# Linear attention into a gated feed-forward layer: k and v of batches 1 and 2 laid out like those of batches 3 to 7

## The chip, the core and the metric

The kernel runs on one core of one Trainium2 chip. The metric is the device time of one execution in microseconds, given as the median of several runs. A profile is one further execution, recorded by the hardware; its times count from the first instruction.

The core has TensorE (PE: matmuls; PEld is its weight load), VectorE (DVE), ScalarE (ACT), GpSimd (POOL) and SyncE (SP). Loads and stores run on 16 DMA engines. In this kernel they are issued from two queues, GpSimd's and SyncE's; only GpSimd's loads also convert float32 to bf16.

## The reference: what is computed

```python
batch, n_heads, seq, head_dim = (8, 8, 576, 64)
theta = pi / 2 * arange(S) / S
phi(x) = concatenate([relu(x) * cos(theta), relu(x) * sin(theta)])   # 64 -> 128 features per token
kv  = einsum('bhsf,bhsd->bhfd', phi(k), v)         # 128 x 64 per head
z   = sum over s of phi(k)
out = einsum('bhsf,bhfd->bhsd', phi(q), kv) / (einsum('bhsf,bhf->bhs', phi(q), z) + 1e-06)

x   = out as 4608 tokens x 512                      # heads side by side
xn  = x / sqrt(mean(x * x) + 1e-06) * rms_g
y   = (silu(xn @ w_gate) * (xn @ w_val)) @ w_out    # 512 -> 1536 -> 512
```

All inputs and the output are float32. The matmuls of the kernel run in bf16.

## The kernel before

Everything is written out by hand in one order per engine (`tc.manual_schedule()`): what stands earlier in the program is issued earlier on its engine, and waits are added only for data and for buffers.

**The feed-forward part** sets the frame. There are nine blocks of 512 tokens, run in the order 0 to 6, 8, 7; block 8 collects the last 64 tokens of each batch. A block has twelve steps (n = 0 to 11). Each multiplies by one 128-column slice of the gate and of the value weights (`half_mm`, L556, into PSUM banks psG and psV), applies silu on ScalarE (L570) and the product on VectorE (L571). Then come four output steps (n = 12 to 15; `out_mm`, L574), followed by the store. Block 0 is cut into smaller units, since its inputs arrive one after another (`unit_mm`, L643). After it, `out_first` runs block 0's output steps with batch 1's attention between the matmuls.

**The attention of batch b** is prepared while the block before it runs. A table of slots says after which step what is done: `at(block, step, where, function, ...)`, with "pe", "mid", "pre" and "post" for the place in the step. For each batch:

- `load_kv` (L107) and `load_q` load k, v and q into a ring of five raw buffers of 128 x 2560 float32.
- `k_phi` (L299) maps k, with the cos half on VectorE (L294) and the sin half on ScalarE (L292), into `kp5`, or into `kp`, which is another view of the same memory.
- `v_cast` (L369) converts v to bf16 into `vv` or `vv5`, each with a column of ones, which gives z.
- `kvz_pe` (L382) multiplies the mapped k by v; `kvz_evac` copies the result out of PSUM.
- `q_phi` and transposes give q with its features on the partitions. Batch 1's first transposes are on TensorE (L363), later ones are DMAs of SyncE's queue (L346).
- `nd_pe` (L449) gives numerator and denominator; `nd_post`, `x_sq`, `x_norm` and `x_tr_dma` (L540) divide, normalize and transpose into the block's input.

**Two layouts of k and v.** `wide(b)` chooses, and is true for batches 3 to 7.

- The nine-token layout (batches 0 to 2): two heads share the 128 partitions, 64 partitions each, and a partition holds nine consecutive tokens of four heads. One load has 128 x 4 pieces of 2,304 bytes. `kvz_pe` needs 4 x 9 x 2 = 72 matmuls with 64 rows (L394); each pair works on the lower and the upper half of the partitions.
- The five-token layout (batches 3 to 7): a partition holds five consecutive tokens of all eight heads, so 115 partitions hold 575 tokens, and the 576th is alone on partition 115. One load has 116 x 8 pieces of 1,280 bytes, issued as two DMAs: rows 0 to 111, then rows 112 to 115 (`KM = 112`; L115). `kvz_pe` needs 4 x 5 x 2 = 40 matmuls with 116 or 115 rows (L387).

Batch 0 has code of its own (`vv0`, `kv0_pe` L430, `z0_pe`), and it uses the nine-token layout directly.

**What sets the order around batches 1 and 2.** GpSimd's queue issues, in this order: q0's first half, v0 in two parts, q0's second half, four pieces of the gate and value weights, k1 (L228), the rest of these weights, q1, v1 (L699), w_out in three parts, k2 (after step 8 of block 0), v2 (step 10). SyncE's queue issues k0 in two parts (L150), and then nothing until batch 1's x is transposed (L540, at 45.9 us). From there on it carries all loads of batches 3 to 7, transposes and stores. Batch 1's k is mapped after steps 5, 6 and 7 of block 0, and its v is cast on GpSimd after step 9 (heads 0 to 3) and on VectorE in step 10 (heads 4 to 7). `kvz_pe(1)` stands in step 11, behind the gate product. Batch 2's k map has four slots (`KCS`, or `KCS5` for the five-token layout) from the output steps of block 0 to step 1 of block 1; its `kvz_pe` is in step 3 of block 1.

Of the kernel before, what the change touches and what calls it, by code (L numbers as in the profile page):

```python
# [10 lines left out]
BF16 = mybir.dt.bfloat16  # L11
# [6 lines left out]
def kernel(  # L18
# [11 lines left out]
    nc = tc.nc  # L30
    B, H, S, D = q.shape
    DM = H * D
    DFF = moe_w_gate.shape[1]
    P = 128
    TB = 512
    HP = H // 2
    NC = S // 64
    NC5 = 5
    KP = S // NC5 + 1
# [3 lines left out]
    E = D + 1  # L43
# [3 lines left out]
    V, A, G = nc.vector, nc.scalar, nc.gpsimd  # L47

    ctx.enter_context(tc.manual_schedule())
    one = ctx.enter_context(tc.tile_pool(name="one", bufs=1))  # L50
# [19 lines left out]
    def kv_rows(src, b, hps):  # L70
        return src[b, 2 * hps[0] : 2 * hps[1], :, :].rearrange(
            "(hp hh) (s c) d -> (hh s) hp (c d)", hh=2, c=NC
        )

    def wide(b):
        return b > 2

    def rows_of(c):
        return KP if c == 0 else KP - 1

    def kv_rows5(src, b, r0, r1):
        part = src[b, :, 0 : NC5 * (KP - 1), :].rearrange(
            "h (p c) d -> p h (c d)", c=NC5
        )[r0 : min(r1, KP - 1)]
        return bass.AP(part.tensor, part.offset, [[NC5 * D, r1 - r0]] + list(part.ap)[1:])
# [6 lines left out]
    def raw_tile(which, b):  # L92
        if (which, b) not in raw:
            t = ring.tile([P, H * NC5 * D], FP32, name="raw", tag="raw")
            raw[(which, b)] = t
        return raw[(which, b)]

    def raw_kv(which, b):
        t = raw_tile(which, b)
        if wide(b):  # L100
            return t[:, :].rearrange("p (h e) -> p h e", h=H)
        return t[:, 0 : HP * NC * D].rearrange("p (hp e) -> p hp e", hp=HP)
# [4 lines left out]
    def load_kv(which, b, hps=(0, HP), eng=nc.sync):  # L107
        src = k if which == "k" else v
        if not wide(b):
            return eng.dma_start(  # L110
                out=raw_kv(which, b)[:, hps[0] : hps[1], :], in_=kv_rows(src, b, hps)
            )
        last = KP if b < B - 1 else KP - 1
        for r0, r1 in ((0, KM), (KM, last)):
            eng.dma_start(  # L115
                out=raw_kv(which, b)[r0:r1, :, :], in_=kv_rows5(src, b, r0, r1)
            )
        if last < KP:
            eng.dma_start(
                out=raw_kv(which, b)[last:KP, :, :].rearrange("p h (c d) -> p h c d", d=D),  # L120
                in_=src[b, :, S - 1 : S, :].rearrange("h s d -> s h d").unsqueeze(2)
                .to_broadcast([1, H, NC5, D]),
            )
# [99 lines left out]
    for i in range(3):  # L223
        m, e = math.frexp(left)
        part.append(math.ldexp(round(m * 256), e - 8))
        left -= part[i]
        G.memset(eps_rows[32 * i : 32 * i + 32, :], part[i] / 32)
    load_kv("k", 1, eng=G)  # L228
    load_w(wg, moe_w_gate, 8, NNT)

# [34 lines left out]
    def cos_of(c):  # L265
# [3 lines left out]
    kp = kp5[:, :, :, :].rearrange("p c h f -> p (c h f)")[:, 0 : NC * HP * F].rearrange(  # L269
        "p (c hp f) -> p c hp f", c=NC, f=F  # L270
    )
    vv = one.tile([P, HP, NC, E], BF16, name="vv")
    vv5 = one.tile([P, H, NC5, E], BF16, name="vv5")
    G.memset(vv[:, :, :, D:E], 1.0)
    G.memset(vv5[:, :, :, D:E], 1.0)
    qpT = one.tile([P, H, TB], BF16, name="qpT")
    xnT = [one.tile([P, NDT, TB], BF16, name=f"xnT{i}") for i in range(2)]
# [6 lines left out]
    def copy(eng, o, i):  # L284
        if eng is A:
            A.copy(out=o, in_=i)  # L286
        else:
            eng.tensor_copy(out=o, in_=i)  # L288
# [10 lines left out]
    def k_phi(eng, b, c, part, hps=(0, HP)):  # L299
        o = slice(0, D) if part == 0 else slice(D, F)  # L300
        f = cos_of if part == 0 else sin_of
        if wide(b):
            rows = rows_of(c)
            src = raw_kv("k", b)[0:rows, :, c * D : (c + 1) * D]
            phi(eng, kp5[0:rows, c, :, o], src, f(14 + c)[0:rows, :])
            return
        src = raw_kv("k", b)[:, hps[0] : hps[1], c * D : (c + 1) * D]
        phi(eng, kp[:, c, hps[0] : hps[1], o], src, f(c))
# [58 lines left out]
        copy(eng, qpT[:, :, j * P : (j + 1) * P], dst)  # L367

    def v_cast(eng, b, hps=(0, HP)):  # L369
        if wide(b):  # L370
            src = raw_kv("v", b).rearrange("p h (c d) -> p h c d", d=D)
            hs = slice(2 * hps[0], 2 * hps[1])
            return copy(eng, vv5[0:KP, hs, :, 0:D], src[0:KP, hs])
        copy(
            eng, vv[:, hps[0] : hps[1], :, 0:D],
            raw_kv("v", b)[:, hps[0] : hps[1], :].rearrange("p hp (c d) -> p hp c d", d=D),
        )

    heads = psA[:, :, 0 : HP * E].rearrange("p g (hp e) -> p g hp e", e=E)
    kvzs = {}  # L380

    def kvz_pe(b):  # L382
        for hp in range(HP):
            for c in range(NC5 if wide(b) else 0):
                for g in range(2):
                    h, r = 2 * hp + g, rows_of(c)
                    nc.tensor.matmul(  # L387
                        heads[:, g, hp, :], lhsT=kp5[0:r, c, h, :], rhs=vv5[0:r, h, c, :],
                        start=(c == 0), stop=(c == NC5 - 1),
                    )  # L390
            for c in range(0 if wide(b) else NC):
                for g in range(2):
                    lo, hi = 64 * g, 64 * g + 64
                    nc.tensor.matmul(  # L394
                        heads[:, g, hp, :], lhsT=kp[lo:hi, c, hp, :], rhs=vv[lo:hi, hp, c, :],
                        start=(c == 0), stop=(c == NC - 1),
                    )


# [277 lines left out]
    lo, hi = (0, NDT // 2), (NDT // 2, NDT)  # L677
# [19 lines left out]
    x_sq(0, 1)  # L697
    load_q(1, eng=G)
    load_kv("v", 1, eng=G)  # L699
    x_norm(0, 0, (0, HALF))  # L700
    x_norm(0, 0, (HALF, DM))
# [51 lines left out]
    def at(blk, n, where, f, *args):  # L753
        slots.setdefault((blk, n), {}).setdefault(where, []).append((f, args))
# [2 lines left out]
        for f, args in slots.get((blk, n), {}).get(where, []):  # L757
            f(*args)

    KCS = ((0, 1, 2), (3, 4), (5, 6), (7, 8))  # L760
    KCS5 = ((0, 1), (2,), (3,), (4,))
    for c in range(NC):
        at(0, 5 + c // 3, "post", k_phi, V, 1, c, 0)
        at(0, 5 + c // 3, "post", k_phi, A, 1, c, 1)
    for j in range(4):
        at(0, (8, 8, 9, 10)[j], "post", q_phi, V, 1, j, 0)
        at(0, (8, 9, 10, 10)[j], "post", q_phi, A, 1, j, 1)
# [1 line left out]
        if j < 2:  # L769
            at(0, 10 + j, "pe", q_tr_pe, 1, j, bank)  # L770
            at(0, 10 + j, "pre", q_tr_evac, V, 1, j, bank)
    at(0, 8, "post", load_kv, "k", 2, (0, HP), G)
    at(0, 9, "post", v_cast, G, 1, (0, 2))
    at(0, 10, "pre", v_cast, V, 1, (2, 4))
    at(0, 10, "post", load_kv, "v", 2, (0, HP), G)

# [19 lines left out]
    def last_step():  # L796
        n = NNT - 1
        g, v = banks_of(0, n)
        run(0, n, "pe")
        half_mm(0, n, wg, g)  # L800
        kvz_pe(1)
        sg = four.tile([P, TB], FP32, name="sg", tag="sg")
        A.activation(out=sg[:, :], in_=g[:, 0:TB], func=AF.Silu)
        kvz_evac(A, 1)
        run(0, n, "pre")
        half_mm(0, n, wv, v)
        nd_pe(1, 0)
        q_tr(2, psV[0])
        nd_post(1, 0)
        V.tensor_tensor(out=hT[:, n, :], in0=v[:, 0:TB], in1=sg[:, :], op=ALU.mult)  # L810
        x_sq(1, 0)
        run(0, n, "post")
# [8 lines left out]
    for nb in range(2, B):  # L821
        b = nb - 1
        first = nb == 2
        for i, cs in enumerate(KCS5 if wide(nb) else KCS):
            kb, kn = ((0, 14), (0, 15), (1, 0), (1, 1))[i] if first else (b - 1, 12 + i)
            for c in cs:
                at(kb, kn, "post", k_phi, V, nb, c, 0)
                at(kb, kn, "post", k_phi, A, nb, c, 1)
        for i in range(2):
            vb, vn = ((0, 15), (1, 0))[i] if first else (b - 1, 13 + 2 * i)  # L830
            at(vb, vn, "post", v_cast, V, nb, (2 * i, 2 * i + 2))
        for j in range(4):
            late = j + (nb == 3)
            qb, qn = (b, 1 + j) if first else (b - (late < 2), (14 + late) % 16)
            at(qb, qn, "post", q_phi, V, nb, j, 0)
            at(qb, qn, "post", q_phi, A, nb, j, 1)
            at(qb, qn, "post", q_tr_dma, nb, j)
        kz = 3 if first else 2
        at(b, kz, "pe", kvz_pe, nb)
        at(b, kz, "pre", kvz_evac, A, nb)  # L840
        for j in range(4):
            n = ((6, 8, 9, 11) if first else (4, 6, 8, 10))[j]
            at(b, n, "mid" if n == 9 else "pe", nd_pe, nb, j)
            at(b, n, "pre", nd_post, nb, j)
            at(b, n, "post", x_sq, nb, j)
            m = n + 2 if first and j == 0 else n + 1
            at(b, m, "post", x_norm, nb, j)
            at(b, m, "post", x_tr_dma, nb, j)

    for pair in range(4):  # L850
        b = 2 * pair or 3
# [9 lines left out]
    for nb in range(3, B):  # L861
        b = nb - 2
# [96 lines left out]
```

## Time and profile before

| | |
|---|---|
| Median of 3 runs | 323.31 us (322.63 to 324.01) |
| Span of the profiled execution | 321.1 us; the page gives no other time of it, and the median is 2.2 us above its span |
| TensorE busy | 313.6 us, 98% |
| VectorE, ScalarE, GpSimd busy | 185.4, 165.8, 40.5 us |
| DMA, SyncE's queue | 41.25 MB, 62.1% of 16 engines' span |
| DMA, GpSimd's queue | 12.13 MB, 15.5% |
| k1 and k2 on GpSimd's queue | 1152 KB each, median 19.2 us from issue to landing |
| v1 and v2 on GpSimd's queue | 1152 KB each, median 15.7 us |
| main k loads of batches 3 to 7, SyncE's queue | 1120 KB each, median 8.8 us |
| granted TensorE clock | 1.000 |

How to read it: the page cuts the span into 40 slices of 8 us and gives each engine's busy share in tenths. The chain that ended last is followed back from the last instruction, and its pieces are work or waiting on the critical path. A timeline line has start, length, engine, line and operation, and in brackets how long the engine had been idle and what ended that. In a table of stretches each engine has its busy time with the number of its instructions, and the last three numbers are the granted clock, the mean busy share of the 16 DMA engines (it can pass 1, since packets of two queues overlap) and the GB/s that arrived. Weights and v0 are converted on the way and count half of what is read.

### The profile page before, as it was taken

To read this page: it belongs to the slowest core of one execution; us is meant where nothing else is said; L and a number is where in the kernel's file an instruction comes from. 1 tells how busy PE (TensorE), PEld (TensorE's weight loads), DVE (VectorE), ACT (ScalarE), POOL (GpSimd) and SP (SyncE) were. 2 spreads that over 40 slices of the span, in tenths; PEclk is the share of its full clock that TensorE was granted. 3 is DMA by queue.
4 is the path that set the end of the run, shared out by engine and by line. 5 is a ranking of instruction groups with operands and counts; after the bars stand their busy time and mean duration, and the time that the engine had idled before them with its cause. 6 is when DMAs were issued, how large, how long until landed. Compare 5 with 4: busy or idle time off the path is not lost.

```text
span 321.1 us, 6023 instructions
## 1 busy us (share of the span) xinstructions
PE 313.6 (98%) x2274; PEld 162.4 (51%) x2310; DVE 185.4 (58%) x382; ACT 165.8 (52%) x322; POOL 40.5 (13%) x79
## 2 busy tenths in 40 slices
PE   7999999999999999999999999999999999999996
PEld 2689564544454445444544445544544444444444
DVE  7976977668457773777457644781676034204410
ACT  5766756754574466554744575446543233223321
POOL 9771211002001100010001100100011000000000
PEclk9999999999999999999999999999999999999999
DMA  7999999788999999999799959995522500041002
GB/s 232 239 270 269 282 329 227 201 183 190 223 226 211 187 263 187 221 247 182 162 186 230 197 163 200 197 217 163 99 59 41 116 33 0 0 102 31 1 35 98
DMA packets 80092, 53.76 MB, mean 167 GB/s; under 512 B 52235, under 2 KB 74047, under 8 KB 80063
## 3 DMA queue, kind: packets, MB, share of 16 engines
q1 hardware_dynamic: 73110, 41.25, 62.1%
q0 software_dynamic: 6944, 12.13, 15.5%
q8 instruction: 18, 0.29, 0.4%
q14 instruction: 12, 0.09, 0.1%
q10 hardware_dynamic: 8, 0.00, 0.0%
HBM read 37.83 MB, written 9.44 MB: 147 GB/s over the span
## 4 chain that ended last, share of the span: by engine, by line
PE 94%; DMA 2%; DVE 1%; issue 1%; POOL 1%; ACT 0%; POOLq 0%; ACTq 0%
PE psC L574 27%; PE psV L556 27%; PE psG L556 26%; PE psV L643 2%; PE psA L449 2%; DMA vv<-in_v_dram 2%; PE psG L574 2%; PE psG L643 2%; PE psA L387 2%; PE psA L394 1%; PE psA L474 0%; PE psV L363 0%; PE psG L430 0%; PE psC L546 0%; POOL raw L135 0%
## 5 line engine op out<-in xcount | busy, mean ns | idle before, releaser
L571 DVE TENSOR_TENSOR hT<-psV,sg 128x512 bf16<-128x512 f32 x99 | 68.2, 689 | 96.5 <-PE psV L556 64.1
L556 PE MATMUL psV<-xnT,wv 128*128 128x512 bf16 x344 | 89.6, 379 | 0.7 <-issue 0.2
L570 ACT ACTIVATE sg<-psG 128x512 f32<-128x512 f32 x99 | 58.6, 592 | 60.8 <-PE psG L556 52.7
L556 PE MATMUL psG<-xnT,wg 128*128 128x512 bf16 x337 | 88.5, 379 | 0.7 <-issue 0.2
L574 PE MATMUL psC<-wo,hT 128*128 128x512 bf16 (+1 forms) x400 | 88.4, 376 | 0.4
L574 PEld LDWEIGHTS <-hT 128*128 128x128 bf16 x456 | 43.1, 98 | 47.7
L556 PEld LDWEIGHTS <-wv 128*128 128x128 bf16 x400 | 39.0, 98 | 46.8
L556 PEld LDWEIGHTS <-wg 128*128 128x128 bf16 x400 | 37.0, 98 | 39.9 <-DVE xnT L288 0.2
L520 POOL TENSOR_TENSOR rs<-ms,mhalf 128x1 f32<-128x1 f32 x36 | 20.5, 570 | 193.9 <-ACT scr L515 193.7
L286 ACT COPY osb<-psC 128x512 f32<-128x512 f32 x32 | 18.7, 585 | 49.9 <-PE psC L574 46.1
L515 ACT ACTIVATE scr<-xt 128x513 bf16<-128x513 f32 x36 | 22.8, 635 | 23.3 <-DVE xt L499 22.3
L527 DVE SCALAR_TENSOR_TENSOR xn<-xt,rs,gb 128x512 bf16<-128x512 f32 (+1 forms) x37 | 26.9, 730 | 9.9 <-POOL rs L520 9.9
L292 ACT ACTIVATE kp<-raw,tab 128x256 bf16<-128x256 f32 (+2 forms) x51 | 28.8, 607 | 2.4 <-DMA raw<-in_k_dram 2.4
L499 DVE TENSOR_TENSOR xt<-psA,rec 128x512 f32<-128x512 f32 x36 | 24.9, 691 | 1.2
L292 ACT ACTIVATE qp<-raw,tab 128x512 bf16<-128x512 f32 (+1 forms) x36 | 23.3, 666 | 1.2 <-DMA raw<-in_q_dram 1.1
L294 DVE TENSOR_SCALAR kp<-raw,tab 128x256 bf16<-128x256 f32 (+2 forms) x53 | 20.1, 428 | 0.5 <-DMA raw<-in_k_dram 0.5
L294 DVE TENSOR_SCALAR qp<-raw,tab 128x512 bf16<-128x512 f32 (+1 forms) x34 | 15.3, 463 | 4.7 <-DMA raw<-in_q_dram 4.7
L449 PEld LDWEIGHTS <-qpT 128*128 128x128 bf16 x224 | 10.6, 97 | 6.6
L556 PE MATMUL psV<-xnT_tail,wv 128*128 128x512 bf16 x48 | 12.3, 379 | 0.1
L556 PE MATMUL psG<-xnT_tail,wg 128*128 128x512 bf16 x46 | 12.0, 379 | 0.1
L288 DVE CAST vv<-raw 116x1280 bf16<-116x1280 f32 (+1 forms) x13 | 11.1, 857 | 1.3 <-DMA raw<-in_v_dram 1.3
L449 PE MATMUL psA<-kvzs,qpT 128*128 128x65 bf16 x224 | 11.4, 193 | 0.0
(102 smaller groups left out, 177.7 us busy)
## 6 DMA issues: line engine op xcount, KB each, us to landing
out_dram<-osb SPq DMA_DIRECT2D x27, 256.0 KB, 2.3
raw<-in_q_dram SPq DMA_DIRECT2D x6, 1024.0 KB, 9.1
raw<-in_k_dram SPq DMA_DIRECT2D x5, 1120.0 KB, 8.8
raw<-in_v_dram SPq DMA_DIRECT2D x5, 1120.0 KB, 9.4
raw<-in_k_dram POOLq DMA_DIRECT2D x2, 1152.0 KB, 19.2
raw<-in_v_dram POOLq DMA_DIRECT2D x2, 1152.0 KB, 15.7
out_dram<-osb SPq DMA_DIRECT2D x17, 128.0 KB, 2.6
wg<-in_moe_w_gate_dram POOLq DMA_DIRECT2D x3, 512.0 KB, 13.8
```

What stands on the lines that cost most here:

```text
L286: A.copy(out=o, in_=i)
L292: A.activation(out=out_ap, in_=in_ap, func=AF.Relu, scale=scale)
L294: eng.tensor_scalar(out=out_ap, in0=in_ap, scalar1=scale, scalar2=0.0, op0=ALU.mult, op1=ALU.max)
L449: nc.tensor.matmul(heads[:, g, hp, :], lhsT=qpT[:, h, j * P : (j + 1) * P], rhs=kvzs[b][:, g, hp * E : (hp + 1) * E], start=True, stop=True,)
L499: V.tensor_tensor(out=xt[:, 0:DM].rearrange("p (hp g d) -> p g hp d", g=2, d=D), in0=heads[:, :, :, 0:D], in1=rec[:, :, :].unsqueeze(3).to ...
L515: A.activation(out=scr[:, :], in_=xt[:, 0 : DM + 1], func=AF.Square, scale=1.0 / math.sqrt(DM), accum_out=ms[:, :],)
L520: G.tensor_tensor(out=rs[:, :], in0=ms[:, :], in1=mhalf[:, :], op=ALU.pow)
L527: V.scalar_tensor_tensor(out=xn_of[(b, j)][:, c], in0=x_of[(b, j)][:, c], scalar=rs_of[(b, j)][:, :], in1=gb[:, c], op0=ALU.mult, op1=ALU. ...
L556: nc.tensor.matmul(bank[:, cols[0] : cols[1]], lhsT=w[:, t, n * P : (n + 1) * P], rhs=x[:, t, cols[0] : cols[1]], start=(t == 0), stop=(t ...
L570: A.activation(out=sg[:, :], in_=g[:, 0:TB], func=AF.Silu)
L571: V.tensor_tensor(out=hT[:, n, :], in0=v[:, 0:TB], in1=sg[:, :], op=ALU.mult)
L574: nc.tensor.matmul(bank[:, 0 : cols[1] - cols[0]], lhsT=hT[:, n, j * P : (j + 1) * P], rhs=wo[:, n, cols[0] : cols[1]], start=(n == 0), st ...
```

## The change

`wide(b)` becomes true for batches 1 and 2. Their k and v are then loaded with five tokens on each of 116 partitions. The first 112 rows stay on GpSimd's queue at the same places in the program, and the DMA for the last four rows goes to SyncE's queue, whichever queue carries the rest. The map of k, the cast of v and `kvz_pe` take the five-token branch, and the tile `vv` and its memset are gone. Batch 1's k map goes from nine pieces over three slots (3, 3, 3) to five (2, 2, 1), batch 2's from (3, 2, 2, 2) to (2, 1, 1, 1).

```diff
     def wide(b):
-        return b > 2
+        return b > 0
...
         for r0, r1 in ((0, KM), (KM, last)):
-            eng.dma_start(
+            (eng if r0 == 0 else nc.sync).dma_start(
                 out=raw_kv(which, b)[r0:r1, :, :], in_=kv_rows5(src, b, r0, r1)
             )
...
-    vv = one.tile([P, HP, NC, E], BF16, name="vv")
     vv5 = one.tile([P, H, NC5, E], BF16, name="vv5")
-    G.memset(vv[:, :, :, D:E], 1.0)
     G.memset(vv5[:, :, :, D:E], 1.0)
...
     def v_cast(eng, b, hps=(0, HP)):
-        if wide(b):
-            src = raw_kv("v", b).rearrange("p h (c d) -> p h c d", d=D)
-            hs = slice(2 * hps[0], 2 * hps[1])
-            return copy(eng, vv5[0:KP, hs, :, 0:D], src[0:KP, hs])
-        copy(
-            eng, vv[:, hps[0] : hps[1], :, 0:D],
-            raw_kv("v", b)[:, hps[0] : hps[1], :].rearrange("p hp (c d) -> p hp c d", d=D),
-        )
+        src = raw_kv("v", b).rearrange("p h (c d) -> p h c d", d=D)
+        hs = slice(2 * hps[0], 2 * hps[1])
+        copy(eng, vv5[0:KP, hs, :, 0:D], src[0:KP, hs])
...
     def kvz_pe(b):
         for hp in range(HP):
-            for c in range(NC5 if wide(b) else 0):
+            for c in range(NC5):
                 for g in range(2):
                     h, r = 2 * hp + g, rows_of(c)
                     nc.tensor.matmul(
                         heads[:, g, hp, :], lhsT=kp5[0:r, c, h, :], rhs=vv5[0:r, h, c, :],
                         start=(c == 0), stop=(c == NC5 - 1),
                     )
-            for c in range(0 if wide(b) else NC):
-                for g in range(2):
-                    lo, hi = 64 * g, 64 * g + 64
-                    nc.tensor.matmul(
-                        heads[:, g, hp, :], lhsT=kp[lo:hi, c, hp, :], rhs=vv[lo:hi, hp, c, :],
-                        start=(c == 0), stop=(c == NC - 1),
-                    )
...
-    KCS = ((0, 1, 2), (3, 4), (5, 6), (7, 8))
     KCS5 = ((0, 1), (2,), (3,), (4,))
-    for c in range(NC):
-        at(0, 5 + c // 3, "post", k_phi, V, 1, c, 0)
-        at(0, 5 + c // 3, "post", k_phi, A, 1, c, 1)
+    for c in range(NC5):
+        at(0, 5 + c // 2, "post", k_phi, V, 1, c, 0)
+        at(0, 5 + c // 2, "post", k_phi, A, 1, c, 1)
...
-        for i, cs in enumerate(KCS5 if wide(nb) else KCS):
+        for i, cs in enumerate(KCS5):
```

## The prediction

> **What bounds the kernel now.** I read the page's busy shares and slices first, then the chain that ended last, then the timeline of the three engines that touch batch 1's k, q and v, then the DMA rate stretch by stretch. The page:
> ```profile
> span 321.1 us, 6023 instructions
> PE 313.6 (98%) x2274; PEld 162.4 (51%) x2310; DVE 185.4 (58%) x382; ACT 165.8 (52%) x322; POOL 40.5 (13%) x79
> DMA  7999999788999999999799959995522500041002
> ```
> TensorE is busy 98%, so time is lost by making it wait or won by giving it less to do. DMA engines are full in the first quarter too: from about 2 to 49 us the weights and batches 0, 1 and 2 pour in behind one another. So a load there is late by everything queued before it. The chain of waits, in three places:
> ```profile
> 3.02 6.81 DMA vv<-in_v_dram
> 9.82 0.04 issue
> 9.87 0.71 PE psG L430 x36
> ...
> 59.43 1.27 PE psA L394 x72
> 60.70 0.16 issue
> 60.85 0.81 PE psG L556 x3
> 61.67 0.86 PE psV L556 x4
> ...
> 91.13 1.23 PE psA L387 x40
> ```
> The reader is to see two things. At 9.87 TensorE starts batch 0's k-times-v on the very landing of v0, with no slack. And L394 (the nine-token form, 72 matmuls) is as long as L387 (the five-token form, 40). From the timeline, batch 1's q and v at the consumer (start, length, idle before it in brackets):
> ```profile
> 34.45 0.72 ACT L292 ACTIVATE qp<-raw,tab 128x512 bf16<-128x512 f32 x1 [0.33 <-DMA raw<-in_q_dram]
> ...
> 37.45 1.15 POOL L288 CAST vv<-raw 128x1152 bf16<-128x1152 f32 x1 [9.66 <-DMA raw<-in_v_dram]
> ...
> 37.79 1.42 DVE L288 CAST vv<-raw 128x1152 bf16<-128x1152 f32 x1
> ```
> q1 and v1 are used as they land, and TensorE wants v1 at 39.56 (L394). The rates (last two columns: share of 16 DMA engines, GB/s):
> ```profile
> core 0: us, PE busy (x) PEld busy (x) DVE busy (x) ACT busy (x) POOL busy (x), PEclk, DMA share, GB/s
> 5.00:6.00 1.00, 0.42 (x4) 0.12 (x4) 0.94 (x2) 0.96 (x3) 1.00 (x3) 1.00 1.11 380
> 30.00:32.50 2.50, 2.50 (x26) 2.23 (x24) 2.20 (x7) 2.46 (x6) 0.00 (x0) 1.00 1.04 351
> 44.50:48.50 4.00, 3.95 (x39) 2.34 (x39) 3.68 (x9) 2.35 (x5) 1.40 (x3) 1.00 1.03 397
> 163.00:167.50 4.50, 4.50 (x36) 2.33 (x35) 2.98 (x7) 2.60 (x6) 0.55 (x1) 1.00 1.34 267
> 196.50:201.00 4.50, 4.50 (x36) 2.34 (x35) 2.42 (x6) 2.37 (x5) 0.55 (x1) 1.00 1.25 266
> 209.50:213.00 3.50, 3.45 (x17) 1.55 (x16) 2.67 (x7) 1.66 (x4) 0.55 (x1) 1.00 1.09 328
> 73.20:73.40 0.20, 0.20 (x2) 0.10 (x1) 0.18 (x1) 0.00 (x0) 0.20 (x1) 1.00 0.65 134
> 73.60:73.80 0.20, 0.20 (x3) 0.10 (x1) 0.20 (x1) 0.00 (x0) 0.00 (x0) 1.00 0.23 51
> ```
> 44.5 to 48.5 is k2 and v2 in the old form (128 rows, 2,304-byte pieces, GpSimd's queue). 163 to 167.5 and 196.5 to 201 each hold one load of the form that the change wants (116 rows, 1,280-byte pieces, SyncE's queue). 30 to 32.5 and 209.5 to 213 are q loads with 128 rows and 1,024-byte pieces, on GpSimd's queue and SyncE's.
>
> **Part 1, the matmuls.** Two batches go from 72 half-height matmuls (L394) to 40 (L387). Counted from the start of the block to the next whole half of a gate or value product: 61.67 - 59.43 = 2.24 us against 93.22 - 91.13 = 2.09 us. So 0.15 us each, 0.3 us in all, and on the path: -0.3.
>
> **Part 2, the vector work.** Batch 1's and 2's k map: 9 x 498 ns on ScalarE becomes 5 x 711 (ScalarE's long qp row; kp tops out at 724), 4.5 to 3.6 us; on VectorE 9 x 346 becomes 5 x about 476, 3.1 to 2.4 us. In the slots they keep, the first holds 3 old or 2 new pieces: 1.29 against about 1.32 us. TensorE waits for neither between 17 and 100 us (its idle pieces there are 0.16 us of issue), so the gain is nothing; if that cover were gone it would be worth at most those 1 us a batch. v's casts grow from 1,152 to 1,280 columns: GpSimd 1.15 to 1.27 us, VectorE 0.75 to 0.82 us. Batch 1's two casts do not overlap: VectorE's takes 1.42 us beside GpSimd's, against 0.75 us at 57 us. The memset of vv (0.27 us at 10.89) goes from GpSimd, which then waits 1.6 us anyway: nothing.
>
> **Part 3, the main loads.** Old: 1.180 MB at 397 GB/s, 2.97 us. New, tail and all: 1.188 MB at 266, 4.47 us. That is the upper end: +1.5 us a load. The lower end is the second piece of k0, which has 1,280-byte pieces on all 128 rows and ran beside GpSimd's q0: 380 GB/s, 3.13 us, +0.16. The queue does not decide it, since q loads run at 351 on GpSimd's queue and 328 on SyncE's; so it is the 112 rows, and I stand near the upper end. Some 0.3 us of the 4.47 is the tail running out (next part), which leaves +1.2 a load. GpSimd pays 0.94 rather than 0.76 us to issue one (its q1 row has 1,024 pieces, the new form 896), twice before v1, in a queue that is full: nothing. [...]
>
> **Part 4, the tails.** Each four-row tail is 41 KB. At 73.2 to 73.8 us batch 3's k load is running out: the share falls to 0.23, which is about 4 engines of 16, at 51 GB/s. So a tail costs between 0.1 us (spread over all at 397 GB/s) and 0.8 us (41 KB at 51 GB/s) on the engines that carry it; I take 0.5 us, the 0.6 us over which that share fell less what the main load still had in it. SyncE's queue is empty from 1.7 to 45.9 us, so the tails go as soon as their buffers are free: k1's and v1's right behind k0, at about 2 us; k2's when k0's last map ends (8.85 us, VectorE); v2's when q0's ends (15.3 us, GpSimd). All four are ahead of q1 and v1, two are ahead of v0, and nothing but k0 is ahead of them. [...] If the four tails meet on the same engines that is +1.0 us for v0 and +2.0 us for v1; both ends kept: 0.2 to 1.6 and 0.4 to 3.2. [...]
>
> **Part 5, the sum.** v0 late by 1.0 us moves TensorE by 1.0 us at once. q1 is late by one load and four tails, 1.2 + 2.0 = 3.2 us; the transposes of q1 want it mapped at 36.1 us and have it at about 35.5, so ScalarE and TensorE are pushed by some 2.6 us, the first 1.0 us among them. v1 is late by 2 x 1.2 + 2.0 = 4.4 us if both add up in full; engines held back by the tails write their rows at another time than the rest and so collide less, and I take 3.6 us (ends: 0.7 and 6.2). After v1's landing (37.43) the two casts need 1.27 + 0.82 us, so the later half of the heads is ready at 39.52 and wanted at 39.56 or, for heads 4 to 7, at 40.18: a slack of 0.04 to 0.66 us, 0.35 taken. TensorE is pushed by 3.6 - 0.35 = 3.25 us. These pushes do not add; the last is the largest. Late next would be w_out's middle third (landed 42.3, wanted 43.4), k2 (47.9, wanted 51.1) and v2 (50.9, wanted 55.4): all move with the ring by 3.6 to 6 us while TensorE has moved by 3.25, so each just holds. The transposes of batch 1's x compete with k2 and v2 for longer (the third, issued 49.62, took 4.3 us, and block 1's first matmul is at 54.1): 0 to 1 us, 0 taken, for they already ran beside full engines. After 60 us nothing differs. Sum: 3.25 - 0.3 = +2.95 us on the span of 321.1. The runs' median, 323.31, is 2.2 us above that span, and I carry those over: 326.2.
>
> **Rivals.** *Loads no slower on GpSimd's queue, tails alone.* No view shows a 112-row load there, and on SyncE's queue transposes were near. Then v1 is late by 0.3 + 2.0 us less the slack 0.35: 2.0 - 0.3 = +1.7 us at most, +0.5 if the tails spread: about 324.4. [...] *It is hidden, and the matmuls' gain stays.* If the rows of a GpSimd load drift apart among the other loads of a full ring, and the tails slip into gaps at the start (share 0.62 to 0.93 between 2 and 3.5 us), v1 is late by less than 0.35 us and v0 not at all: -0.3 us, 323.0. It decides from v1's lateness: under 0.65 us the kernel is not slower. Against it stands a share above 1.0 all the way to 37 us. *Faster by over 0.5%* would need 1.6 us of TensorE's time, and parts 1 and 2 show 0.3: only if the maps' relief of ScalarE counts where no wait is shown.
>
> **How the numbers follow.** v1 late (forecast): 0.60, its own range 324.9 to 328.2. Tails alone: 0.22, half of it above 324.9. Hidden: 0.14. Faster: 0.04. What this kernel's measurements can tell from no change is about 0.5%, 1.6 us. Slower by more: 0.60 + 0.11, say 0.70; within: 0.26; faster: 0.04. The range goes from 323.2, which leaves out most of the hidden case, to 328.0.
>
> **What would show it.** Right: GpSimd's cast of v1 starts near 41 us, with TensorE idle before the first five-token block or just before q1's transposes; v0 lands near 10.8; the rate falls below 300 GB/s for some 4 us around 22 to 25 and again after 36 us. Part 1 is right if batch 2's block gives 2.09 us. Wrong: k1 and v1 pass at over 380 GB/s, or v0 lands at 9.8 as before, so that the tails cost nothing; or v1 comes late but GpSimd's and VectorE's casts hide it.

## The result and the profile after

The changed kernel takes 334.18 us (333.54 to 334.35) against 323.31 us (322.63 to 324.01): 1.0332 times as long, 95% interval 1.0314 to 1.035. That is 10.9 us slower; the forecast was 2.9 us slower, and its range ended at 328.0. Of the four executions the profiled one had a mean granted clock of 0.999 and took 333.54 us; the other three had 0.983 to 0.990 and took 334.04 to 334.35 us.

The page of the changed kernel, the lines that answer to those shown of before:

```profile
span 331.8 us, 5892 instructions
PE 316.3 (95%) x2210; PEld 162.6 (49%) x2246; DVE 184.8 (56%) x374; ACT 164.9 (50%) x314; POOL 41.1 (12%) x78
DMA  8999999978999999999699958995821310041002
```

TensorE's share falls from 98 to 95%: it now waits. Where, its own timeline says. These are the changed kernel's TensorE rows with an idle time before them of 0.5 us or more after the first loads (start, length, line, tiles; in brackets the idle time before and what ended it):

```profile
12.50 0.71 PE L416 MATMUL psG<-vv,kp 64*128 64x64 bf16 x36 [1.72 <-DMA vv<-in_v_dram]
...
17.07 0.81 PE L361 MATMUL psV<-ident,qp 128*128 128x128 bf16 x8 [0.54 <-ACT qp L290]
...
43.10 0.62 PE L361 MATMUL psC<-ident,qp 128*128 128x128 bf16 x8 [2.91 <-ACT qp L290]
...
49.56 1.39 PE L380 MATMUL psA<-vv,kp 116*128 116x65 bf16 x40 [2.80 <-POOL vv L286]
```

The answering pieces of the kernel before, from its chain that ended last (start, length, line):

```profile
36.08 0.45 PE psC L363 x8
...
39.56 1.27 PE psA L394 x72
```

The reader can follow the lateness by these rows. Batch 0's k-times-v starts at 12.50 instead of 9.87 us: 2.6 us. Batch 1's q is transposed at 43.1 instead of 36.1: 7.0 us. Its k-times-v (L380, before L394) starts at 49.56 instead of 39.56: 10.0 us, and that goes through to the end, where the span is 10.7 us longer. So the loss is made before 50 us, in two places: before v0, where the new main loads play no part yet (GpSimd issues k1 only at 11.49 us), and between v0 and v1. What ended the waits for batch 1, in the changed kernel's timeline of ScalarE and GpSimd:

```profile
42.33 0.72 ACT L290 ACTIVATE qp<-raw,tab 128x512 bf16<-128x512 f32 x1 [4.34 <-DMA raw<-in_q_dram]
...
47.60 1.90 POOL L286 CAST vv<-raw 116x1280 bf16<-116x1280 f32 x1 [13.35 <-DMA raw<-in_v_dram]
```

q1 is there at 42.3 instead of 34.4 us, v1 at 47.6 instead of 37.4. And the rates, as a table of stretches (last three columns: granted clock, share of the DMA engines, GB/s), the first while v0 is under way, the second while k2 and v2 are:

```profile
6.00:8.50 2.50, 2.50 (x20) 1.02 (x18) 0.45 (x3) 0.74 (x3) 2.46 (x6) 1.00 1.15 100
50.00:56.00 6.00, 5.89 (x86) 4.06 (x85) 3.89 (x10) 2.90 (x7) 0.86 (x2) 1.00 1.09 229
```

The same two stretches of the kernel before:

```profile
6.00:8.50 2.50, 2.50 (x26) 1.17 (x25) 2.50 (x8) 2.45 (x6) 2.50 (x5) 1.00 1.10 272
44.50:48.50 4.00, 3.95 (x39) 2.34 (x39) 3.68 (x9) 2.35 (x5) 1.40 (x3) 1.00 1.03 397
```

The engines are as busy as before and move 100 GB/s instead of 272, and 229 instead of 397. A busy share does not tell here how many bytes flow: 1.15 stands beside 100 GB/s, 1.10 beside 272. Nor does it pass 1 only where packets of two queues overlap: in the kernel before it is 1.25, at 207 GB/s, between 13 and 17 us, and SyncE's queue issues nothing from 1.7 to 45.9 us.

### The profile page after: what moved, and what is told of

It is laid out like the page before. It is cut to its first block, busy times and chain, and to the rows that moved or that the text cites. A ratio compares the mean times of both kernels' runs of the same rounds, so it can differ in the third digit from the quotient of the medians.

```text
span 331.8 us, 5892 instructions
## 1 busy us (share of the span) xinstructions
PE 316.3 (95%) x2210; PEld 162.6 (49%) x2246; DVE 184.8 (56%) x374; ACT 164.9 (50%) x314; POOL 41.1 (12%) x78
## 4 chain that ended last, share of the span: by engine, by line
PE 82%; DMA 11%; issue 5%; POOL 1%; DVE 1%; POOLq 0%
PE psV L542 25%; PE psC L560 25%; PE psG L542 25%; DMA raw<-in_k_dram 6%; DMA raw<-in_q_dram 3%; PE psA L380 3%; PE psA L435 2%; PE psG L560 1%; DMA xnT<-xn 1%; POOL vv L286 1%; PE psA L460 0%; PE psV L361 0%; POOL raw L115 0%; DVE xt L485 0%; DVE xn L513 0%
## 5 line engine op out<-in xcount | busy, mean ns | idle before, releaser
L284 ACT COPY osb<-psC 128x512 f32<-128x512 f32 x32 | 18.7, 585 | 49.9 <-PE psC L560 45.9
L290 ACT ACTIVATE kp<-raw,tab 115x512 bf16<-115x512 f32 (+2 forms) x43 | 27.8, 677 | 5.0 <-DMA raw<-in_k_dram 5.0
L292 DVE TENSOR_SCALAR qp<-raw,tab 128x512 bf16<-128x512 f32 (+1 forms) x34 | 16.0, 483 | 9.5 <-DMA raw<-in_q_dram 9.5
L292 DVE TENSOR_SCALAR kp<-raw,tab 115x512 bf16<-115x512 f32 (+2 forms) x45 | 18.9, 461 | 2.5 <-DMA raw<-in_k_dram 2.5
L286 DVE CAST vv<-raw 116x1280 bf16<-116x1280 f32 x13 | 10.7, 822 | 3.6 <-DMA raw<-in_v_dram 3.6
L380 PE MATMUL psA<-vv,kp 116*128 116x65 bf16 (+1 forms) x280 | 9.8, 193 | 2.8 <-POOL vv L286 2.8
```

The lines of the kernel that those rows point to most:

```text
L290: A.activation(out=out_ap, in_=in_ap, func=AF.Relu, scale=scale)
L292: eng.tensor_scalar(out=out_ap, in0=in_ap, scalar1=scale, scalar2=0.0, op0=ALU.mult, op1=ALU.max)
L380: nc.tensor.matmul(heads[:, g, hp, :], lhsT=kp5[0:r, c, h, :], rhs=vv5[0:r, h, c, :], start=(c == 0), stop=(c == NC5 - 1),)
```

## The experiments

At the start stood theory A, two separate causes (the early four-row loads on SyncE's queue, and slow 112-row loads), against B, one cause (those four-row loads put some DMA engines behind for good). "Before" was between 323.09 and 323.31 us in all comparisons. "Tails" are the DMAs of rows 112 to 115.

| run | us | ratio to before, 95% interval |
|---|---|---|
| tails on GpSimd's queue | 329.27 and 330.86; 334.45 and 335.40 | 1.019 and 1.024 for the first two, no interval |
| only two early tails added to before | 327.97 | 1.0131 to 1.0172 |
| one early tail added to before | 324.34 | 1.0023 to 1.0051 |
| two early tails, to spread rows | 323.90 | 1.0009 to 1.003 |
| changed kernel without tails | 329.04 | 1.0135 to 1.0196 |
| before, loads cut at row 112 | 331.54 | 1.0237 to 1.0294 |
| before, loads cut at row 64 | 334.83 | 1.0327 to 1.0401 |
| before, loads cut into even and odd rows | 327.17 | 1.0082 to 1.0157 |
| changed, 128 overlapping rows | 323.72 | 1.0012 to 1.003 |
| changed, 128 rows, whole | 323.51 | 0.9999 to 1.0021 |
| the same, v1's casts swapped | 323.35 | 1.0 to 1.0017 |
| only batch 2 changed | 329.29 | 1.0165 to 1.0209 |
| only batch 2, 128 rows | 323.86 | 1.0012 to 1.0031 |

**The early tails alone.** To the kernel before, two loads were added on SyncE's queue behind k0:

```diff
+    for spare, src in ((wo, k), (hT, v)):
+        to = spare[:, :, :].rearrange("p n s -> p (n s)").bitcast(FP32)[KM:KP, 0 : H * NC5 * D]
+        nc.sync.dma_start(
+            out=to.rearrange("p (h e) -> p h e", h=H), in_=kv_rows5(src, 1, KM, KP)
+        )
```

> The kernel before, with two four-row loads added on SyncE's queue behind k0: the tails of k1 and v1 in the new form, written to rows 112 to 115 of buffers that are not in use yet (w_out's and h's). They are read by nobody, and all else is as before. Theory A: the first loads are held up as in the changed kernel (v0 at about 12.5 us instead of 9.8), and about 3 us of it reaches the end: 325.5 to 327.5 us. Rival B: nearly all of the 10.9 us, 331 to 334 us. If two tails cost only the bytes they move, 0.2 to 1.0 us: 323.5 to 324.3 us.

It took 327.97 us, 4.9 us more than before, for 82 KB. v0 lands as late as in the changed kernel. From the chain that ended last, this run:

```profile
3.02 9.25 DMA vv<-in_v_dram
12.27 0.04 issue
12.31 1.16 PE psG L436 x36
```

v0's landing (3.02 + 9.25) is at 12.27 instead of 9.83. That is 2.4 us, and the kernel loses twice that. Where the rest is lost, the third line shows: the 36 matmuls take 1.16 instead of 0.71 us. The table of stretches of this run says why: the granted clock is 0.50 from 9 to 15 us, where it is 1.00 in the kernel before.

```profile
9.00:15.00 6.00, 4.74 (x62) 3.16 (x59) 3.36 (x10) 3.08 (x8) 2.06 (x5) 0.50 1.14 255
```

So A's forecast of the place holds. Its range ended at 327.5 us; it had no term for the clock. B falls here: 4.9 us is not nearly all.

**One tail instead of two** (only `((wo, k),)` in the loop above):

> The kernel before with one early four-row load on SyncE's queue (k1's rows 112 to 115 only) instead of two. [...] If any such load costs a fixed hold-up: as with two, 327.5 to 328.5 us.

324.34 us; v0 landed at 10.7 us, 0.9 us late, and the clock stayed at 1.00. So the hold-up is not a fixed one: it grows with the bytes, 0.9 us for 41 KB and 2.4 us for 82. The loss at the end grows faster, 1.1 and 4.9 us; with two tails the clock is also 0.50 from 9 to 15 us.

**The same tails to other rows.** Same source, queue, place and bytes; only the destination differs. If the hold-up stays, it does not come from the rows that are written:

```diff
-.bitcast(FP32)[KM:KP, 0 : H * NC5 * D]
+.bitcast(FP32)[64:80:4, 0 : H * NC5 * D]
```

> The kernel before with the same two early four-row loads on SyncE's queue as in the run that adds only early tails: same source rows, same bytes, same queue and place, but written to rows 64, 68, 72 and 76 instead of 112 to 115. [...] If it is that few engines carry them behind k0 (D), nothing changes: v0 at 12.3, 327.5 to 328.5 us.

323.90 us, v0 at 10.3 us, and the stretch that fell to 110 GB/s with rows 112 to 115 runs at 250. First the run with neighbouring rows, then this one:

```profile
6.00:8.50 2.50, 1.99 (x18) 0.82 (x16) 0.64 (x4) 0.93 (x3) 2.50 (x5) 1.00 1.15 110
```

```profile
6.00:8.50 2.50, 2.50 (x24) 1.06 (x24) 1.92 (x6) 2.20 (x6) 2.50 (x5) 1.00 1.05 250
```

So D falls: that few engines carry the tails costs at most the 0.5 us by which v0 is still late. What costs, about 2 of the 2.4 us, is that the four rows are neighbours on the write side. That it matters which rows are written at the same time is C in what follows, and it holds for the tails.

**The main loads without tails.** The changed kernel, with rows 112 to 115 of batches 1 and 2 neither loaded nor used:

```diff
-        for r0, r1 in ((0, KM), (KM, last)):
+        for r0, r1 in ((0, KM), (KM, last))[: 1 if b < 3 else 2]:
```

> The changed kernel without the tails of batches 1 and 2: rows 112 to 115 (tokens 560 to 575 of those batches) are neither loaded nor used, so those 16 tokens are missing from the sums over k and v. The 112-row loads on GpSimd's queue are as in the changed kernel. If these loads alone are slow (A): v0 lands at 9.8 us, v1 4 to 6 us after 37.4, 327 to 331 us. If the tails are the whole loss (B): 323 to 323.5 us.

329.04 us. v0 is on time (9.84), v1 is there at 42.5 instead of 37.4, and the rate while k2 and v2 load is 236 GB/s:

```profile
46.00:54.00 8.00, 7.72 (x76) 4.64 (x76) 4.92 (x12) 4.23 (x8) 1.11 (x2) 0.86 1.06 236
```

So A holds: the 112-row loads cost 5.8 us without any tail. Part of that goes with the clock, which is 0.50 from 45 to 48 us here: the one of four executions that kept a mean clock of 1.000 took 326.81 us, the three with 0.995 took 328.83 to 329.47.

The 5.8 us and the 4.9 us of the early tails add up to 10.7 of the 10.9 us, but that is partly luck. Both contain a fallen clock, which the changed kernel's profile does not show. And there GpSimd casts v1 10.2 us late, while it does so 5.1 us late without tails and 2.8 us late with the early tails alone. Some 2.3 us of v1's lateness are in neither run, and no run separates them. The two later tails by themselves are not enough: in the run with only batch 2 changed (below) they go at 9.2 and 15.6 us, and v1 is cast 0.5 us late.

**Tails on GpSimd's queue** (`eng.dma_start` for both pieces):

> The changed kernel, but the four-row tails of batches 1 and 2 go on GpSimd's queue right behind their 112 rows. Theory A (two causes: the early tails on SyncE's queue hold up the first loads, and the 112-row loads themselves are slow): v0 lands at 9.8 us again and batch 0's k-times-v starts at 9.9 instead of 12.5, but v1 still lands 5 us or more after 37.4, so the kernel stays slower than the one before: 328 to 331 us. Rival B (one cause: the tails on SyncE's queue put some DMA engines behind for good, and the 112-row loads run at the old rate): the whole loss goes with them, 323 to 324.5 us.

The start is as before (TensorE begins batch 0's k-times-v at 9.83), which again puts that loss on SyncE's early tails, but the kernel stays slow: 329.27 us in the profiled execution, and 330.86, 334.45 and 335.40 us in the others, where A gave 328 to 331. That these tails cost more than leaving them out is not shown, for the profiled execution without tails took 329.25 us. The run has a wait of its own, though, which the cuts below share.

**Old layout, cut rows.** To see whether the 112 rows or the 1,280-byte pieces make the loads slow, the kernel before got its loads of batches 1 and 2 in two parts, pieces unchanged:

```diff
-            return eng.dma_start(
-                out=raw_kv(which, b)[:, hps[0] : hps[1], :], in_=kv_rows(src, b, hps)
-            )
+            full = kv_rows(src, b, hps)
+            for r0, r1 in ((0, KM), (KM, P)):
+                eng.dma_start(out=raw_kv(which, b)[r0:r1, hps[0] : hps[1], :], in_=full[r0:r1])
+            return
```

> The kernel before, with each load of k and v of batches 1 and 2 cut into rows 0 to 111 and rows 112 to 127, both on GpSimd's queue, with the old pieces of 2,304 bytes and the old layout. If it is the 112 rows that make the loads slow, then k1 and v1 move at about 260 GB/s instead of 397, v1 lands 2 to 4 us late and the kernel takes 325 to 327.5 us. If it is the 1,280-byte pieces on GpSimd's queue, the rate stays above 380 GB/s and the kernel takes 323 to 324 us.

331.54 us, and 233 GB/s while k2 and v2 load, both parts of a load taken together:

```profile
48.00:55.00 7.00, 7.00 (x74) 4.06 (x69) 4.54 (x12) 3.86 (x8) 1.11 (x2) 0.92 1.07 233
```

Pieces of 2,304 bytes are as slow as those of 1,280 (236 GB/s without tails), if the load is cut at row 112. The other half of the test, the changed kernel with 1,280-byte pieces on 128 rows:

```diff
+        if b < 3:
+            part = src[b, :, 0 : NC5 * (KP - 1), :].rearrange("h (p c) d -> p h (c d)", c=NC5)
+            rows = bass.AP(part.tensor, part.offset, [[4 * D, P]] + list(part.ap)[1:])
+            return eng.dma_start(out=raw_kv(which, b), in_=rows)
```

> The changed kernel, but k and v of batches 1 and 2 are loaded by one DMA each on GpSimd's queue with 1,280-byte pieces on all 128 rows: the rows start four tokens apart, so they overlap and hold other tokens than they should, and the attention of batches 1 and 2 is left wrong in that; sizes of all other work are as in the changed kernel. There are no tails. If it is the 112 rows, these loads run at about 380 GB/s (1.31 MB in 3.4 us, 0.5 us more than before each) and the kernel takes 323 to 324.5 us. If it is the 1,280-byte pieces, they run at about 240 GB/s as in the changed kernel and it takes 328 us or more.

323.72 us, at 371 GB/s:

```profile
44.50:50.00 5.50, 5.50 (x54) 3.13 (x52) 4.93 (x13) 2.96 (x8) 1.67 (x3) 1.00 1.03 371
```

So it is the rows. The loss of the run cut at 112 is larger than theory A gave (325 to 327.5 us), and the next two runs tell part of the reason. With halves, `((0, 64), (64, P))`:

> The kernel before, with each load of k and v of batches 1 and 2 cut into rows 0 to 63 and rows 64 to 127, both on GpSimd's queue, old pieces and layout. [...]

and with the same number of rows, loads and bytes, but even rows in one and odd rows in the other:

```diff
+            for r0 in range(2):
+                eng.dma_start(out=raw_kv(which, b)[r0:P:2, hps[0] : hps[1], :], in_=full[r0:P:2])
```

> The kernel before, with each load of k and v of batches 1 and 2 cut into its 64 even rows and its 64 odd rows, both on GpSimd's queue. Number of loads, rows, pieces and bytes are those of the run with rows 0 to 63 and 64 to 127 (334.8 us, about 216 GB/s while k2 and v2 load); only which rows go together differs. If the write side decides, by which neighbouring rows are written at the same time (C), each half now reaches all groups of rows, the rate comes back to 300 GB/s or more and the kernel takes 323 to 327 us. If it is the number of rows or of loads, whatever rows they are (E), nothing changes: 333 us or more.

334.83 and 327.17 us. While k2 and v2 load, first with rows 0 to 63 and 64 to 127, then with even and odd rows:

```profile
49.00:56.00 7.00, 6.95 (x64) 3.93 (x63) 6.35 (x16) 4.13 (x9) 1.67 (x3) 1.00 1.03 216
```

```profile
44.50:48.50 4.00, 4.00 (x46) 2.58 (x45) 2.80 (x8) 1.82 (x4) 0.56 (x1) 1.00 1.02 391
```

216 against 391 GB/s: E falls, and C's forecast holds for the main loads too, though here the rows that are read change along with the rows that are written. v1 is cast at 37.6 us with even and odd rows, as in the kernel before. The 327.17 us lie just above C's 327, and most of the loss that is left, 2.36 of 3.9 us, has another place. GpSimd's and TensorE's timelines of that run:

```profile
23.87 0.79 POOL L190 DMA_DIRECT2D wo<-in_moe_w_out_dram  x1 [2.04 <-DMA wv<-in_moe_w_val_dram]
...
26.09 0.40 PE L547 MATMUL psC<-ident,xn 128*128 128x128 bf16 x4 [2.36 <-DVE xn L528]
```

Where a load on GpSimd's queue waits for a landing in these traces, it is that of the eighth load before it: k2 2.49 us for k1 in the kernel before, w_out's first piece 2.04 us for a piece of the value weights here. Cutting k1 and v1 puts two more loads in front of w_out's, so that wait falls earlier (on w_out's first piece, where the kernel before has it on the third). GpSimd stands still for 2 us, and behind it in its order stands `rs` (L521), which VectorE needs for batch 0's x and TensorE after it. The runs with tails on GpSimd's queue (2.12 us at 25.85), cut at 112 (1.85 us at 25.62) and cut at 64 (3.04 us at 26.74) have the same hole. The even-and-odd run is therefore what the cut ones are to be compared with: neighbouring rows cost 4.4 us at 112 and 7.7 us at 64. These prices include a fallen clock, 0.995 and 0.990 on average in the profiled executions of the two cut runs against 1.000 with even and odd rows.

**A form without 112 rows and without tails.** Five tokens a partition on all 128 rows, rows 116 to 127 running on into the next head's tokens and read by nobody:

```diff
+        if b < 3:
+            part = src[b, :, 0 : NC5 * (KP - 1), :].rearrange("h (p c) d -> p h (c d)", c=NC5)
+            rows = bass.AP(part.tensor, part.offset, [[NC5 * D, P]] + list(part.ap)[1:])
+            return eng.dma_start(out=raw_kv(which, b), in_=rows)
```

> The changed kernel with one DMA on GpSimd's queue for each k and v of batches 1 and 2, over all 128 rows with five tokens each: rows 0 to 115 hold what they should, rows 116 to 127 run on into the next head's tokens and are read by nobody. No tails, 1.31 MB instead of 1.19. All is computed. If row count and tails are the whole loss (A and C): as the run with overlapping rows, 323.2 to 324.2 us. If that run was quick only because its source rows overlapped, so that less was fetched: 325 us or more.

323.51 us, not distinguishable from before. This is the change with its whole loss taken out. The 0.3 us of shorter matmuls does not show. In this run v1 (1.31 instead of 1.18 MB a load) is cast 0.8 us later, at 38.2 us; GpSimd's cast takes 1.90 us there, beside VectorE's, which went first, and TensorE waits 0.95 us for it. With the two casts swapped (GpSimd heads 4 to 7):

> The run with whole 128-row loads for batches 1 and 2, with the two casts of v1 swapped: VectorE casts heads 0 to 3, GpSimd heads 4 to 7. In that run VectorE's cast came first and held GpSimd's, which took 1.9 us and made TensorE wait 0.9 us for the first heads. If this was what ate the matmuls' 0.3 us: 322.5 to 323.3 us, at or a little under the kernel before. If v1's landing itself is the limit: no change, 323.3 to 323.8 us.

323.35 us, ratio 1.0 to 1.0017. That is at the lower edge of "no change" and 0.05 us above the other range. TensorE's wait for the casts is down from 0.95 to 0.34 us, though v1 is cast 0.7 us later in this profile. So what ate the 0.3 us is not settled. No version beat the kernel before.

**Only batch 2.** `wide(b)` as `b > 1`, loads as in the change:

> Only batch 2 is changed as in the changed kernel (112 rows on GpSimd's queue, tails on SyncE's); batch 1 keeps its nine-token form. Its tails go when k0's and q0's buffers are free, after v0. If a late load matters only where its user is next (A): k2 and v2 have 3 us or more to spare, the start is as before, and the kernel takes 322.9 to 324 us. If every 112-row load costs its lateness in full: 326 us or more.

329.29 us: my expectation was wrong by 5 us, though k2 and v2 have time to spare. What is late is another transfer. TensorE's timeline of this run:

```profile
57.84 1.55 PE L556 MATMUL psG<-xnT,wg 128*128 128x512 bf16 x3 [3.35 <-DMA xnT<-xn]
59.18 1.91 PE L556 MATMUL psV<-xnT,wv 128*128 128x512 bf16 x4
60.89 1.39 PE L556 MATMUL psG<-xnT,wg 128*128 128x512 bf16 x4
62.11 1.03 PE L556 MATMUL psV<-xnT,wv 128*128 128x512 bf16 x4
```

The transpose of batch 1's x runs beside the slow load and takes 7.85 us (in the chain, from 49.86); block 1 waits 3.35 us for it. Then four matmuls take 1.91 us instead of 1.03: the granted clock is 0.55 between 58 and 60 us. In the changed kernel the same wait is only 0.34 us, probably since TensorE is 10 us late by then and the load nearly through. With batch 2's load over 128 rows instead:

> Only batch 2 in the five-token form, loaded by one DMA each over 128 rows (rows 116 to 127 run on into the next head and are read by nobody); batch 1 as in the kernel before. In the run with 112 rows and tails for batch 2 alone, TensorE waited 3.35 us for the transposes of batch 1's x. If those waited only for the slow load (A), that wait is gone, and what stays is the 0.15 us of shorter matmuls: 322.8 to 323.7 us. If the five-token form itself holds the transposes up: 326 us or more.

323.86 us, a little above what I expected. Most of the wait is gone with the slow load, but 1.33 us of it stays, beside loads of 1.31 instead of 1.18 MB; no run shows whether these bytes are the reason.

## Why the prediction was wrong

**The places were right. Of the two prices, that of the tails failed in kind and that of the main loads in size.** The prediction named v0, q1's map and v1's cast as the points where TensorE would be pushed, and gave 10.8 us for v0 and about 41 us for the cast of v1; measured were 12.5 and 47.6.

- *Part 1, matmuls, -0.3 us*: right. Batch 2's block runs from 69.94 to the next whole half at 72.04 us: 2.10 us against 2.09 forecast and 2.24 before. No run shows the gain at the end, though.
- *Part 4, tails*: this step failed in kind. It priced a tail by the engines that carry it (0.5 us each on four of 16) and took all else to run on. In fact two early tails slow every transfer: 100 GB/s for 2.5 us, v0 2.4 to 2.6 us late against 1.0 forecast and 1.6 as the upper end, and by themselves 4.9 us at the end, a clock of 0.50 for 6 us included. The rows decide it: with the same tails on rows 64, 68, 72 and 76, v0 is only 0.5 us late. The changed kernel shows no such stretch for the two tails that go later, at 10.2 and 19.0 us. That the tails meet on the same engines, from which the 1.0 and 2.0 us were summed, no run shows; the runs show 0.9 us of v0's lateness for one early tail and 2.4 us for two.
- *Part 3, main loads*: right kind, mis-sized. Forecast +1.2 us a load with +1.5 as the upper end. Measured on GpSimd's queue: 2 x 1.147 MB at 229 GB/s take 10.0 us where 2 x 1.180 MB at 397 took 5.9, so +2.0 us a load. The 266 GB/s of SyncE's loads, from which the price came, were taken for the form's rate on any queue since the queue had made little difference for q's 128-row loads (351 and 328 GB/s). For 112 rows the two differ: 266 there, 229 to 236 here. No run separates the queue from what else runs beside the loads.
- *Part 5, the sum*: "these pushes do not add" was half right. The ring's lateness grows from point to point (2.6, 7.0, 10.0 us), and the end is the last of them, as forecast. That engines held back by the tails collide less, by which v1's 4.4 us became 3.6, no run shows; v1 was 10.2 us late. And the slack of 0.35 us at v1's casts was not there: with v1 late, VectorE's cast went first, GpSimd's took 1.90 us instead of the 1.27 that the sum took, and TensorE waits for that one. And the clock was left out. It stayed at 1.00 in the changed kernel's stretches shown above, but fell in its other three executions, and in the profiled ones of the runs with early tails alone, without tails, with tails on GpSimd's queue, with loads cut at 112 and 64, and with batch 2 alone (mean 0.990 to 0.995).
- *x's transposes, 0 taken of 0 to 1 us*: 0.34 us in the changed kernel, probably because it was late already; 3.35 us with batch 2 alone.

The rival "hidden" falls with the row rates. The rival "tails alone" had its place right for the start (early tails do cost by themselves), but gave 0.5 to 1.7 us where they cost 4.9, and the main loads are slow on GpSimd's queue after all (229 to 236 GB/s). Its 0.5 us for spread tails was the author's estimate; no run spreads them over other engines.

**What stays open.** That neighbouring rows on the write side make transfers slow is shown for the tails, since only the destination's rows were changed. For the 64-row loads the grouping of the rows is shown to decide, but it changes on the read side as well, so that it is the write side is inferred. Why 112 rows (229 to 236 GB/s) are nearly as slow as 64 (216) was not shown: no view tells which engine writes which rows. Nor was it settled why the run with tails on GpSimd's queue varies from 329 to 335 us, where the 2.3 us of v1's lateness come from that neither part of the change has alone, and when the clock falls.

## What to carry to other kernels

When a load does not cover all 128 partitions, take its price from a run or a trace row of exactly that row range and queue, not from its bytes; reading a little too much on 128 rows (1.31 instead of 1.19 MB) was 10.7 us faster here than 112 rows and a tail of four. A small load is not cheap because it is small (two early tails, 82 KB together, cost 4.9 us here): where the DMA engines are full and something waits for the next landing, look at which rows it writes and what is in flight beside it. And before a load is cut in two, count the loads on its queue: here two more made GpSimd wait for a landing, and work behind it was late by 2 us.

## What the runs showed of the hardware

- Two four-row loads to neighbouring rows (82 KB) brought 16 engines from 272 down to 100 to 110 GB/s for some 2.5 us, their busy share staying at 1.15. Written to rows four apart, the same bytes left 250 GB/s.
- 64 neighbouring rows at a time: 216 GB/s. The same rows taken as even and odd: 391 GB/s.
- A TensorE wait of 3.35 us was followed by a granted clock of 0.55 from 58 to 60 us (only batch 2 changed). But 2.52 us were followed by 0.50 for 3 us (without tails), and 2.12 us by 0.57 for 4 us (tails on GpSimd's queue). With early tails alone the clock was 0.50 from 9 to 15 us, and TensorE's longest wait from 1.2 us to there had been 0.77 us. Waits of 2.91 and 2.80 us in the changed kernel's profile, and of 2.36 us with even and odd rows, left it at 1.00. So no length of a wait separates, in these runs, those that kept the clock from those that lost it.
- VectorE's and GpSimd's casts into the same tile hardly overlapped. In the kernel before, VectorE's came second (37.79 after 37.45 us) and took 1.42 us, against 0.75 us at 57 us. In the changed kernel GpSimd's came second (47.60 after 47.57 us) and took 1.90 us. With loads cut at 112, GpSimd's took 1.73 instead of 1.15 us for the same shape.
